# Nine pairs of chunks instead of five with the up product from 15 products of thirds

## The chip, the cores and the metric

The kernel runs on one core of one Trainium2 chip. The metric is device time in microseconds (us) of one execution. The profile of one execution is read beside it: when each instruction ran on each engine, and what ended each wait.

## The reference

The program is a gated linear recurrence followed by a mixer. Batch is 4, heads 8, sequence 768, head size 48; all data are float32. The recurrence, with the complex gate `a` limited to a magnitude of 0.999:

```python
for t in range(S):
    ar, ai = (a_re_n[:, :, t, :, None], a_im_n[:, :, t, :, None])
    new_re = ar * S_re - ai * S_im
    new_im = ar * S_im + ai * S_re
    kv = np.einsum('bhd,bhe->bhde', k[:, :, t], v[:, :, t])
    S_re, S_im = (new_re + kv, new_im)
    y[:, :, t] = np.einsum('bhd,bhde->bhe', q[:, :, t], S_re)
```

Its output, heads side by side, is `x` with 768 tokens of 384 numbers per batch. The mixer:

```python
xt = x.transpose(0, 2, 1)
h = xt @ U @ V                                  # over the tokens, rank 32
u = x + h.transpose(0, 2, 1)
ch = np.maximum(u @ w_ch1, 0.0) @ w_ch2         # 384 -> 1536 -> 384
return (u + ch).astype(np.float32)
```

## The kernel before

**Tiling.** The tokens are cut into 24 chunks of 128 (6 to a batch). Attention works on chunks. Two chunks form a gate group (12 groups, 0 to 11), and from group 5 on the products of a group's two chunks are issued together. The mixer works on pairs of chunks, `m` = 0 to 11, three to a batch. Since the rank product needs a batch's six chunks, a batch's mixing follows its attention and runs beside the attention of the next batch.

**Order.** Nothing is scheduled at run time. Every step is added to a plan with its engine and a stage, and the table `ORDER` gives each step, by engine and stage, its place in one long list (2671 places). The steps are issued in that order; each engine then works in order and waits on semaphores. The table `SPARE` puts fill matmuls of the identity, which compute nothing that is used, ahead of some places (`idle`, L1519; one unit is 128 columns, and a fill is left out where no PSUM tile is free).

**Gates.** ScalarE and VectorE turn a group's gates into magnitudes and angles (`magnitudes_of`, `turns_of`, `angles`, `waves`), with the tables of ScalarE switched twice a group. The sign of the real part becomes 1/pi with that sign, by bit operations on VectorE (L678), for the groups in `BITS` (0 to 2); for groups 3 to 11 ScalarE takes a Sign (with the constant `tiny`), and a second ScalarE step scales the angle and adds a quarter (with `fourth`). From group 3 on the values are split into two rounded parts for TensorE (`GS`). Sums over blocks of tokens ("tot", L741) and prefix products ("es ps", "ef ps", "ph") go through TensorE.

**Attention of a chunk.** `prep` weights queries and keys (`qk`), multiplies them by cosine and sine into `QKC` (two tiles, each head's two halves of 48 padded to 64 columns, so that a head takes 112 rows once transposed: `DQ` = 64 + 48). TensorE transposes them ("tr", L860), ScalarE copies them to `QK` (L871), of which there are three tiles. `chain` then scales `QK` in place by decays (`T`, VectorE), forms the blocks of the attention matrix ("inner", "corners"), the states ("dk", L996, `G`, `GM`), and reads out `y` (L1027, L1035) into `xo`, of which there are eight tiles.

**Mixing of a pair.** The rank product, `mixed` onto `xo`, a transpose to `uT` (L1107, L1111), then the up product into `h`, then the down product:
- *Up, plain* (`up`, L1122): pairs 0 to 6. Six steps, each with two row blocks of the weight and three parts of the contraction, 36 matmuls of 256 columns. ScalarE reads each step's PSUM with a relu into `h`.
- *Up, by thirds* (`up_fewer`, L1222): from pair `FEWER` = 7 on. The weight is cut into 3 x 3 blocks and `uT` into 3 x 2, and 15 products of sums of such blocks give the six thirds of the output. Each product is four matmuls of 128 columns. Four chains of partial sums run in PSUM (A and B long, C, D, E short). After every product its third is read: by a ScalarE copy the first time (L1230), later by VectorE, which adds it onto `h` (L390) and takes the relu with the last one (L1234). VectorE forms the twelve sums of `uT` for each pair in `put` (L1194) and once, in `combine` (L1275), eight sums of weight blocks. Both kinds of sum are kept in the `GATE` area, which the gates no longer need by then, with two weight sums in `sums_w`.
- *Down* (`down`, L1313, for pair 0; `down_two`, L1356, for the others): seven products of halves with sums `S1`, `S2` that VectorE forms (L1348) in `HS`: four pieces left over in `stage` (three) and `more`. The results are added to `xo` (L390) and stored.

One mixing step of the down product is half a product, 0.98 us in the plan's own costs.

Of the kernel before, what the change touches and what calls it, by code (L numbers as in the profile page):

```python
# [18 lines left out]
CH = 128  # L19
# [20 lines left out]
        ("POOL", "load"): {0: [14], 1: [34], 1.5: [84], 2: [31]},  # L40
        ("DVE", "load"): {1: [58]},
# [6 lines left out]
        ("ACT", "gates"): {0: [1, 2, 4, 6, 7, 16, 17, 22, 23, 29, 28, 45, 70, 71], 1: [24, 27, 38, 39, 41, 42, 46, 47, 65, 64, 67, 68], 2: [129, 108,  # L48
# [10 lines left out]
        ("DVE", "gates"): {0: [5, 8, 13, 18, 19, 54, 49], 1: [30, 21, 40, 43, 44, 51, 50], 2: [111, 143, 156, 185, 169], 4: [277, 322, 323, 372, 356],  # L59
# [10 lines left out]
        ("ACT", "angles"): {0: [72, 86, 98, 100, 103], 1: [76, 106, 112, 114, 126], 2: [210, 231, 251, 240, 241, 242, 263, 269, 271], 4: [375, 395,  # L70
# [5 lines left out]
        ("DVE", "angles"): {0: [81, 89], 1: [87, 107], 2: [211, 232, 252], 4: [376, 402, 425], 6: [589, 597, 602, 612, 625, 626, 665], 8: [698, 716,  # L76
# [4 lines left out]
        ("DVE", "prep"): {0: [85, 104, 110], 1: [121, 128, 145], 2: [226, 250, 265], 3: [203, 304, 309], 4: [373, 424, 427], 5: [443, 470, 472], 6:  # L81
# [159 lines left out]
def kernel(  # L241
# [19 lines left out]

    nc = tc.nc
    B, H, S, D = q.shape
    DP = 64
    DQ = DP + D
    DM = H * D  # L270
    FF = moe_w_ch1.shape[1]
    R = moe_U.shape[1]
    KD = DM // 128
# [78 lines left out]
    def c_one(n):  # L352
        return 0.15 + 0.00052 * n
# [1235 lines left out]
```

## Time and profile before

| | us |
|---|---|
| runs (3) | 627.15, 628.55, 629.3; median 628.55 |
| profiled execution, from first to last instruction | 627.0 |
| TensorE busy (PE) | 609.9 |
| TensorE weight loads (PEld) | 526.2 |
| VectorE busy (DVE) | 499.7 |
| ScalarE busy (ACT) | 415.8 |
| GpSimd busy (POOL) | 38.1 |

The profiled execution has no time of its own beside its span; the runs are measured from outside the span. PE counts matmuls, whose ends are modelled, so that neighbours overlap and the row of a group is longer than its share of the time; PEld counts the loads of the fixed operand, which run under earlier matmuls. A row of a group reads: line, engine, operation, output<-input, shape, count | busy us, mean ns of one | idle time before it, and what ended that. A row of the timeline reads: start, duration, line, operation, count of instructions merged into the row. A row of the waits reads: who waited for whom: us in total, times, longest. f32 matmuls are two instructions each.

### The profile page before, as it was taken

The numbers are of one execution on the slowest core, as the hardware profiler recorded it, in microseconds if no ns is written. First come the engines' busy times: TensorE is split into PE (matmuls) and PEld (weight loads), VectorE is DVE, ScalarE is ACT, GpSimd is POOL, SyncE is SP. The second block draws the span as 40 slices with busy tenths as digits, with TensorE's granted clock in tenths as the row PEclk, the third lists the DMA queues.
The fourth block names the chain that finished last, engine by engine and source line by source line (L and its number), as shares of the span: only waits on it lengthen the run. The fifth ranks groups of instructions, "written<-read, shape, count | busy, mean of one in ns | idle before, by whom it ended". The sixth has DMA issues, their size and how long they took to land.

```text
span 627.0 us, 23447 instructions
## 1 busy us (share of the span) xinstructions
PE 609.9 (97%) x10380; PEld 526.2 (84%) x10380; DVE 499.7 (80%) x887; ACT 415.8 (66%) x807; POOL 38.1 (6%) x79
## 2 busy tenths in 40 slices
PE   6998989999999999999999999999999999999998
PEld 3566767666889889889989989888999998999997
DVE  6899999888999979758977867788989884464554
ACT  6999999999898988687787867688433431202010
POOL 5000000000001010010000100000100100000100
PEclk7999999999999999999999999999999999999999
DMA  8864565644143252541512512601203020000101
GB/s 211 191 146 115 135 136 132 155 111 104 33 80 76 50 120 44 99 89 28 99 37 46 113 40 46 124 19 25 63 21 60 9 51 3 1 1 1 45 14 44
DMA packets 173685, 45.74 MB, mean 73 GB/s; under 512 B 167632, under 2 KB 170384, under 8 KB 173584
## 3 DMA queue, kind: packets, MB, share of 16 engines
q1 hardware_dynamic: 171376, 39.90, 30.1%
q0 software_dynamic: 2208, 4.35, 2.1%
q8 instruction: 81, 1.33, 0.9%
q14 instruction: 20, 0.16, 0.1%
HBM read 33.59 MB, written 4.72 MB: 61 GB/s over the span
## 4 chain that ended last, share of the span: by engine, by line
PE 77%; ACT 4%; DVE 3%; DMA 1%; issue 1%; SPq 0%; ACTq 0%; DVEq 0%
PE down L1356 24%; PE up L1122 15%; PE few L1222 11%; PE dk L996 3%; PE tr L860 3%; PE y L1035 3%; PE inner L910 2%; PE down L1313 2%; PE inner L907 2%; PE tot L741 2%; PE y L1027 2%; PE mixed L1089 2%; PE es ps L692 1%; PE ef ps L692 1%; PE uTp L1107 1%; PE corners L971 1%
## 5 line engine op out<-in xcount | busy, mean ns | idle before, releaser
L1122 PE MATMUL up<-uT,w 128*128 128x256 f32 x504 | 116.9, 383 | 0.0
L387 DVE TENSOR_TENSOR QK<-QK,T 112x512 f32<-112x512 f32 (+2 forms) x144 | 102.1, 732 | 8.4 <-PE inner L910 4.3
L1122 PEld LDWEIGHTS up<-uT,w 128*128 128x128 f32 x504 | 93.6, 190 | 12.5
L1356 PE MATMUL down<-w,h 128*128 128x192 f32 x396 | 72.2, 331 | 0.0
L384 ACT ACTIVATE gate<-gate 128x768 f32<-128x768 f32 (+1 forms) x82 | 64.8, 795 | 7.4 <-DVE GS L791 3.2
L1356 PEld LDWEIGHTS down<-w,h 128*128 128x128 f32 x396 | 64.1, 190 | 1.5 <-issue 0.7
L871 ACT COPY QK<-tr 112x512 f32<-112x512 f32 x96 | 51.2, 590 | 14.6 <-PE tr L860 14.3
L390 DVE TENSOR_TENSOR xo<-down,xo 128x192 f32<-128x192 f32 (+1 forms) x79 | 29.9, 387 | 27.5 <-PE down L1356 27.0
L387 DVE TENSOR_TENSOR QKC<-qk,cs 128x768 f32<-128x768 f32 x44 | 41.7, 955 | 6.3 <-ACT cs L384 3.6
L1230 ACT COPY h<-few 128x512 f32<-128x512 f32 x30 | 17.2, 586 | 40.8 <-PE few L1222 40.8
L1356 PE MATMUL down<-stage 128*128 128x192 f32 x198 | 37.6, 331 | 0.0
L1111 ACT COPY uT<-uTp 128x384 f32<-128x384 f32 x22 | 10.0, 479 | 41.4 <-PE uTp L1107 26.9
L1222 PE MATMUL few<-gate,w 128*128 128x128 f32 x280 | 34.8, 275 | 0.0
L1298 POOL DMA_DIRECT2D out_dram<-xo x32 | 19.2, 644 | 243.3 <-DVE xo L390 140.0
L860 PEld LDWEIGHTS tr<-ident,QKC 64*112 64x112 f32 x768 | 24.5, 130 | 10.7 <-issue 4.7
L1222 PEld LDWEIGHTS few<-gate,w 128*128 128x128 f32 x280 | 33.3, 192 | 0.0
L1356 PEld LDWEIGHTS down<-stage 128*128 128x128 f32 x198 | 32.1, 190 | 0.7 <-issue 0.2
L779 POOL DMA_DIRECT2D gate<-F x15 | 12.0, 799 | 327.9 <-DVE w L578 113.5
L860 PE MATMUL tr<-ident,QKC 64*112 64x64 f32 x768 | 29.4, 221 | 2.3 <-DVE QKC L387 1.6
L381 ACT ACT_TABLE_LOAD x24 | 30.8, 1283 | 1.1 <-PEq L1573 0.7
L384 ACT ACTIVATE h<-up 128x512 f32<-128x512 f32 x42 | 24.6, 596 | 9.8 <-PE up L1122 9.5
L976 ACT COPY AT<-corners 32x128 f32<-32x128 f32 x96 | 24.2, 255 | 9.6 <-PE corners L971 8.3
(200 smaller groups left out, 1285.4 us busy)
## 6 DMA issues: line engine op xcount, KB each, us to landing
stage<-in_moe_w_ch_dram SPq DMA_DIRECT2D x12, 768.0 KB, 5.0
qk<-in_q_dram SPq DMA_DIRECT2D x24, 192.0 KB, 3.2
qk<-in_k_dram SPq DMA_DIRECT2D x24, 192.0 KB, 2.7
VP<-in_v_dram SPq DMA_DIRECT2D x24, 192.0 KB, 3.6
gate<-in_a_re_dram SPq DMA_DIRECT2D x22, 192.0 KB, 3.4
gate<-in_a_im_dram SPq DMA_DIRECT2D x22, 192.0 KB, 3.4
AT<-DG SPq DMA_DIRECT2D x96, 32.0 KB, 2.3
T<-E SPq DMA_DIRECT2D x48, 48.0 KB, 2.9
```

The lines of the kernel that those rows point to most:

```text
L381: ACT(1.37, rank, lambda: nc.scalar.preload_act_table_set(name), writes=[TABLE])
L384: return nc.scalar.activation(out=o, in_=i, func=f, **kw)
L387: nc.vector.tensor_tensor(out=o, in0=a, in1=b, op=OP.mult)
L390: nc.vector.tensor_tensor(out=o, in0=a, in1=b, op=OP.add)
L860: nc.tensor.transpose(out=get(*ps[r])[0:DQ, h], in_=get(*qkc)[at, h].rearrange("p u d -> p (u d)")[:, 0:DQ], identity=ident[at, at], tile_ ...
L871: nc.scalar.copy(out=to, in_=a)
L976: ACT(0.36, RR, lambda r=r, u=u: nc.scalar.copy(out=get(*ATi).rearrange("p (a u) t -> p a u t", u=2)[r:r + BLK, :, u, BLK:2 * BLK], in_=ge ...
L996: nc.tensor.matmul(out=get(*dk[r])[x:end, h], lhsT=get(*ks)[at, h, x // DP, 0:end - x], rhs=get(*VPi)[at, h], start=True, stop=True, tile_ ...
L1122: nc.tensor.matmul(out=get(*ps)[:, e], lhsT=w1[:, f, (ff + e) * 128:(ff + e + 1) * 128], rhs=get(*uT)[:, f], start=(f == 0), stop=(f == KD ...
L1222: nc.tensor.matmul(out=get(*ps)[:, q], lhsT=w()[:, q * 128:(q + 1) * 128], rhs=v[0](), start=(n == 0 and q == 0), stop=True, skip_group_ch ...
L1298: queue.dma_start(out=out[b, c * CH:(c + 1) * CH, lo:hi], in_=get("xo", i)[:, lo:hi])
L1356: nc.tensor.matmul(out=get(*to)[:, part], lhsT=x(j), rhs=y[:, j], start=(first and j == 0), stop=(j == KH - 1), skip_group_check=not first)
```

## The change

1. `FEWER` = 3: pairs 3 to 11 form the up product by thirds, so four more pairs than before, 3 to 6.
2. Since the gates still need `GATE` at that time, the twelve operand sums go to `HS`, the tiles of the down product's sums, three to a piece. Seven of the eight weight sums go to `sums_w`, which grows from two to seven rows, and the eighth onto a block of `w1` that is not read any more; `combine` forms them in a slightly changed sequence.
3. The room comes from `QK`: two tiles instead of three, and 96 rows instead of 112. `QKC` holds a head's two halves of 48 next to each other (`DQ` = 96), with a short zeroed strip at the end, and the tiles `T` are no longer filled with ones at the start.
4. All groups take the sign by bits on VectorE. The ScalarE step that scaled the angle and added a quarter is gone: the quarter is added in the rounding steps (`angles`).
5. New code for `SUMMED` groups is there, but `SUMMED` is empty.
6. `ORDER` is new from the second batch's gates on (2770 places); `SPARE` loses its entries at places 514 to 551 and 664 to 678, 63 units in all; ten of these stood at places 514 and 518, ahead of group 3's block totals.

Places of some steps in the list:

| | before | after |
|---|---|---|
| transposes of chunk 14 | 1463, 1464 | 1509 on |
| last read-out of chunk 12, of chunk 13 | 1449, 1491 | 1483, 1533 |
| mixing of pair 3 | 1296 to 1502 | 1317 to 1504 |
| mixing of pair 6 | 1925 to 2122 | 2012 to 2159 |
| weight sums | 2018 to 2125 | 813 to 1287 |
| last read-out of chunk 23 | 2410 | 2512 |
| mixing steps of pair 8 ahead of it (of 29) | 20 | 22 |

The diff without `ORDER`:

```diff
-    DQ = DP + D
+    DQ = 2 * D
-    FEWER = B * (S // CH) // 2 - 5
+    FEWER = 3
...
-        QKC.append(singles.tile([128, H, 2, DP], FP, name="QKC%d" % n))
-        nc.gpsimd.memset(QKC[n][:, :, :, D:DP], 0.0)
+        QKC.append(singles.tile([128, H * DQ + DP - (DQ - DP)], FP, name="QKC%d" % n))
+        nc.gpsimd.memset(QKC[n][:, H * DQ:], 0.0)
...
-    sums_w = singles.tile([128, 2, KF // 3 * 128], FP, name="sums")
+    sums_w = singles.tile([128, 7, KF // 3 * 128], FP, name="sums")
...
-        nc.gpsimd.memset(TS[n], 1.0)
...
-            if g in BITS:
-                DVE(c_one(W), R1, lambda: nc.vector.tensor_scalar(out=t(n).bitcast(U32), in0=t(ar).bitcast(U32), scalar1=0x80000000,
-                                                                  scalar2=INV_PI, op0=OP.bitwise_and, op1=OP.bitwise_or), AR, [N])
-            else:
-                ACT(ca + 0.09, R1, lambda: act(t(n), t(ar), AF.Sign, bias=tiny), AR, [N])
+            DVE(c_one(W), R1, lambda: nc.vector.tensor_scalar(out=t(n).bitcast(U32), in0=t(ar).bitcast(U32), scalar1=0x80000000,
+                                                              scalar2=INV_PI, op0=OP.bitwise_and, op1=OP.bitwise_or), AR, [N])
...
-            if g not in BITS:
-                ACT(ca + 0.09, R2, lambda: act(t(z), t(z), AF.Identity, scale=1.0 / math.pi, bias=fourth), [], Z)
...
-                    ACT(c_act(DM), R2, lambda: nc.scalar.copy(out=of(a, i), in_=of(z, i)), [zi], [a + (i,)])
+                    ACT(c_act(DM) + 0.09, R2, lambda: act(of(a, i), of(z, i), AF.Identity, bias=fourth), [zi], [a + (i,)])
...
-                DVE(c_dve(DM), R2, lambda: nc.vector.tensor_tensor(out=of(b, i), in0=of(z, i), in1=of(a, i).bitcast(FP), op=OP.subtract),
-                    [zi, a + (i,)], [b + (i,)])
+                DVE(c_dve(DM), R2, lambda: nc.vector.scalar_tensor_tensor(out=of(b, i), in0=of(z, i), scalar=0.25, in1=of(a, i).bitcast(FP),
+                                                                          op0=OP.add, op1=OP.subtract), [zi, a + (i,)], [b + (i,)])
...
+    def turns_of_heads(qkc):
+        return get(*qkc)[:, 0:H * DQ].rearrange("p (h u d) -> p h u d", u=2, d=D)
...
-        buffer(QK, "QK", 3, [DQ, 5, H * HC])
+        buffer(QK, "QK", 2, [DQ, 5, H * HC])
...
         def mix_of(n):
-            return GATE[:, n, 0:KF // 3 * 128] if n < 6 else sums_w[:, n - 6]
+            return sums_w[:, n] if n < 7 else w1[:, 2, 0:KF // 3 * 128]
...
             def x(n, w=1):
-                at = n3 * 128 + n // 6 * CH
-                return GATE[:, n % 6, at:at + CH] if w == 1 else GATE[:, n:n + w, at:at + CH] if n < 6 else GATE[:, n - 6:n - 6 + w, at:at + CH]
+                a = HS[(2, 0, 1, 3)[n // 3]]
+                return a[:, n % 3] if w == 1 else a[:, n % 3:n % 3 + w]
 
             def x_of(n):
-                return "few", n % 6, "x%d" % (n // 6)
+                return "hs", (2, 0, 1, 3)[n // 3], n
...
-                S1, S2 = ("s1", 0, half), ("s2", 0, half)
+                S1, S2 = ("hs", half), ("hs", 2 + half)
```

More of the change, by code (lines that the diff above doesn't have):

```diff
@@ L171 @@
-        ("POOL", "angles"): {6: [615], 8: [708, 733], 10: [882, 931], 12: [1097], 14: [1273, 1302], 16: [1472, 1516], 18: [1669], 20: [1879, 1913],
-        22: [2039, 2077]},
-        ("DVE", "mixing"): {7: [2018, 2019, 2021, 2030, 2032, 2024, 2040, 2102, 2108, 2115, 2120, 2125, 2027]},
[7 rows of a table added]
+        ('POOL', 'load'): {0: [14], 1: [34], 1.5: [84], 2: [31]},
+        ('DVE', 'load'): {1: [58]},
[6 rows of a table added]
+        ('ACT', 'gates'): {0: [1, 2, 4, 6, 7, 16, 17, 22, 23, 29, 28, 45, 70, 71], 1: [24, 27, 38, 39, 41, 42, 46, 47, 65, 64, 67, 68], 2: [129, 108,
[10 rows of a table added]
@@ L174 @@
+        2003], 6: [2341, 2221, 2344], 7: [2419, 2302, 2436], 8: [2650, 2603, 2620], 9: [2656, 2618, 2658], 10: [2722, 2680, 2698]},
+        ('POOL', 'angles'): {6: [614], 8: [706, 731], 10: [861, 900], 12: [1076], 14: [1258, 1285], 16: [1505, 1565], 18: [1771], 20: [1950, 1976],
+        22: [2218, 2270]},
+        ('DVE', 'mixing'): {3: [930, 992, 1074, 1091, 1101, 813, 1006, 1031, 1126, 1279, 1283, 1284, 1287]},
 }
 SPARE = {20: 8, 32: 9, 62: 1, 66: 1, 73: 1, 82: 5, 91: 1, 113: 6, 116: 1, 119: 8, 140: 8, 153: 6, 157: 4, 167: 1, 168: 1, 207: 6, 216: 1, 217: 1, 282:
-         1, 352: 2, 436: 1, 514: 5, 518: 5, 527: 4, 546: 4, 547: 25, 551: 12, 596: 2, 601: 1, 606: 3, 624: 1, 632: 3, 646: 1, 653: 1, 664: 1, 672: 2,
@@ L301 @@
     PL = H * HC
-    BITS = range(SPLIT[0])
     PUT = (0, 2), (4, 6), (8, 10)
@@ L443, in w2_of @@
         return w2.rearrange("p (j x) m -> p j x m", x=2)[:, :, x, y * DH:(y + 1) * DH]
-    leps, lmax, tiny = column("leps", math.log(1e-6)), column("lmax", LNMAX), column("tiny", 1e-30)
+    leps, lmax = column("leps", math.log(1e-6)), column("lmax", LNMAX)
     magic, fourth, quarter = column("magic", MAGIC), column("fourth", 0.25), column("quarter", math.pi / 2)
@@ L655, in magnitudes_of @@
             table(ca, R1, lambda: act(t(y), t(y), AF.Ln, bias=1.0), [], Y)
-            if on_dve:
+            if g in SUMMED or g in SPREAD:
                 DVE(c_one(W), R1, lambda: nc.vector.tensor_scalar(out=t(l), in0=t(l), scalar1=-0.5, scalar2=-LNMAX, op0=OP.mult,
                                                                   op1=OP.max), [], [L])
-                DVE(cd, R1, lambda: add(t(l), t(l), t(y)), Y, [L])
+                if g not in SUMMED:
+                    DVE(cd, R1, lambda: add(t(l), t(l), t(y)), Y, [L])
             else:
@@ L685, in within @@
         def within(i, R1, L):
-            ps, es = ("es ps", i), ("es", i)
+            ps, es, parts = ("es ps", i), ("es", i), (y, l) if g in SUMMED else (l,)
             def summed(m, name, to, keeps):
@@ L695, in summed, with each @@
                 else:
-                    PE(0.65, R1, lambda: nc.tensor.matmul(out=get(*to), lhsT=m.bitcast(FP), rhs=of(l, i), start=True, stop=True),
-                       [L, name], [to, ("sums", g, i)], takes=[keeps], steps=2)
+                    def each():
+                        for u, a in enumerate(parts):
+                            nc.tensor.matmul(out=get(*to), lhsT=m.bitcast(FP), rhs=of(a, i), start=(u == 0), stop=(u == len(parts) - 1))
+                    PE(0.65 * len(parts), R1, each, [L, name] + [y + (i,)] * (g in SUMMED), [to, ("sums", g, i)], takes=[keeps], steps=2 * len(parts))
             psum(ps, "T", [128, DM], [128, 512])
@@ L726, in of_blocks @@
             lo = first
-            ps, e = ("tot", i), ("E", g)
+            ps, e, parts = ("tot", i), ("E", g), (y, l) if g in SUMMED else (l,)
             psum(ps, "T", [128, HH, NTOT])
@@ L734, in sums @@
                         h, w = at + (u * HH + p) * D, 64 if u == 0 else D
-                        nc.tensor.matmul(out=get(*ps)[u * 64:u * 64 + w, p], lhsT=get(*l)[:, h:h + w], rhs=total, start=True,
-                                         stop=True, tile_position=(0, u * 64))
+                        for n, a in enumerate(parts):
+                            nc.tensor.matmul(out=get(*ps)[u * 64:u * 64 + w, p], lhsT=get(*a)[:, h:h + w], rhs=total, start=(n == 0),
+                                             stop=(n == len(parts) - 1), tile_position=(0, u * 64))
             def at_once():
@@ L744, in of_blocks @@
             else:
-                PE(0.51, R1, sums, [l, ("total", 0), ("sums", g)], [ps], way=1, takes=[e], steps=4 * HH)
+                PE(0.2 + 0.31 * len(parts), R1, sums, [l, ("total", 0), ("sums", g)] + [y + (i,)] * (g in SUMMED), [ps], way=1, takes=[e],
+                   steps=4 * HH * len(parts))
             used = 2 * D if g in SPLIT else 64 + D
@@ L994, in state @@
                     at = slice(r * HC, (r + 1) * HC)
-                    for x, end in ((0, DP), (DP, DQ)):
-                        nc.tensor.matmul(out=get(*dk[r])[x:end, h], lhsT=get(*ks)[at, h, x // DP, 0:end - x], rhs=get(*VPi)[at, h],
+                    for x, w in ((0, DP), (DP, D)):
+                        nc.tensor.matmul(out=get(*dk[r])[x:x + w, h], lhsT=get(*ks)[at, h * DQ + x:h * DQ + x + w], rhs=get(*VPi)[at, h],
                                          start=True, stop=True, tile_position=(r * HC, x))
@@ L1169, in mix_of @@
         def mix_of(n):
-            return GATE[:, n, 0:KF // 3 * 128] if n < 6 else sums_w[:, n - 6]
+            return sums_w[:, n] if n < 7 else w1[:, 2, 0:KF // 3 * 128]
         def c_of(n):
-            return ("few", n, "w") if n < 6 else ("few", 0, "w%d" % n)
+            return "sums_w", n
         def up_fewer():
@@ L1275, in put @@
                 DVE(c_dve(n3), RC, lambda: nc.vector.tensor_tensor(out=c(n), in0=x(), in1=y(), op=op),
-                    [("w1", f) for f in range(KD)] + [c_of(k) for k in reads], [c_of(n)] + [("few", "b")] * (n == 3))
+                    [("w1", f) for f in range(KD)] + [c_of(k) for k in reads], [c_of(n)] + [("w1", 2, 0)] * (n == 7))
             sub_, add_ = OP.subtract, OP.add
@@ L1382, in down_two @@
             onto(ub, 0, two, 1)
-            product(one, 0, lambda j: of_s(2, j), W2S[1], lambda half: [("s2", 0, half)], first=False)
+            product(one, 0, lambda j: of_s(2, j), W2S[1], lambda half: [("hs", 2 + half)], first=False)
             onto(ua, 1, one, 0)
@@ L1388, in down_two @@
             sums(3, 1)
-            product(two, 0, lambda j: of_s(0, j), W2S[0], lambda half: [("s1", 0, half)])
+            product(two, 0, lambda j: of_s(0, j), W2S[0], lambda half: [("hs", half)])
             onto(ub, 1, two, 0)
@@ L1394, in down_two @@
             leave(0, 0)
-            product(two, 0, lambda j: of_s(2, j), w2_of(1, 1), lambda half: [("s2", 0, half)], first=False)
+            product(two, 0, lambda j: of_s(2, j), w2_of(1, 1), lambda half: [("hs", 2 + half)], first=False)
             onto(ua, 1, two, 0)
@@ L1467 @@
                 ring((nm, i), nm, EF)
-            ring(("few", n), nm, EF)
-            ring(("few", "b"), nm, EF)
-        else:
-            ring(("few", n), "g" + nm, [GATE[:, n]])
     waits, later, done = [], [], 0
```

56 lines of the change are left out of this document (27 added, 29 removed), and 246 rows, old and new, of the table ORDER.

## The prediction

> **What bounds the kernel now.** I read the page first: its busy line, then the chain that ended last.
>
> ```profile
> span 627.0 us, 23447 instructions
> PE 609.9 (97%) x10380; PEld 526.2 (84%) x10380; DVE 499.7 (80%) x887; ACT 415.8 (66%) x807; POOL 38.1 (6%) x79
> PE 77%; ACT 4%; DVE 3%; DMA 1%; issue 1%; SPq 0%; ACTq 0%; DVEq 0%
> PE down L1356 24%; PE up L1122 15%; PE few L1222 11%; PE dk L996 3%; PE tr L860 3%; PE y L1035 3%; PE inner L910 2%; PE down L1313 2%; PE inner L907 2%; PE tot L741 2%; PE y L1027 2%; PE mixed L1089 2%; PE es ps L692 1%; PE ef ps L692 1%; PE uTp L1107 1%; PE corners L971 1%
> ```
>
> TensorE carries the chain and is busy nearly always, but a busy TensorE may be pipelining slowly, so next I asked what TensorE itself waited for. The two longest entries:
>
> ```profile
> PE es ps L696 <- DVE GL L390: 3.8, 1, 3.8
> PE tr L860 <- DVE QKC L387: 1.6, 4, 0.8
> ```
>
> The 3.8 us is one wait at the start; everything else is a microsecond or two. Then I cut the span into stretches, because the engines do not share the load evenly. The columns are length, busy time of each engine, granted clock, DMA share and GB/s; 526 us is where the last chunk's read-out ends.
>
> ```profile
> core 0: us, PE busy (x) PEld busy (x) DVE busy (x) ACT busy (x) POOL busy (x), PEclk, DMA share, GB/s
> 20.00:120.00 100.00, 93.19 (x2168) 68.52 (x2166) 97.67 (x153) 96.55 (x188) 0.00 (x0) 1.00 0.60 143
> ...
> 160.00:220.00 60.00, 60.00 (x1280) 53.80 (x1279) 57.05 (x94) 54.40 (x107) 2.66 (x4) 1.00 0.33 64
> ...
> 440.00:526.00 86.00, 86.00 (x1758) 81.47 (x1758) 75.32 (x149) 31.59 (x77) 4.08 (x7) 1.00 0.17 37
> 160.00:526.00 366.00, 365.61 (x7070) 329.42 (x7070) 303.37 (x534) 256.17 (x513) 22.34 (x35) 1.00 0.30 59
> 526.00:626.00 100.00, 97.97 (x747) 94.75 (x742) 50.29 (x114) 14.34 (x28) 4.81 (x9) 1.00 0.05 17
> ```
>
> Three regimes. Up to 120 us VectorE (97.67 of 100) and ScalarE (96.55) are the limit. From 160 to 526 us attention and mixing run together and TensorE is the limit (365.61 of 366), with VectorE at 303.37/366 = 82.9%. In the tail only the mixer is left: TensorE full, VectorE half idle. Pairs 3 to 6, whose up product changes, lie in the middle regime. So TensorE work saved there is time saved, as long as VectorE, which pays for it, stays under its limit.
>
> **The up product, on TensorE.** Two pieces of the chain, each an unbroken run of one kind, with the time and the number of instructions:
>
> ```profile
> 325.83 7.77 PE up L1122 x36
> ...
> 463.96 7.14 PE few L1222 x64
> ```
>
> An `up` instruction (256 columns) takes 7.77/36 = 0.216 us, a `few` instruction (128 columns) 7.14/64 = 0.1116 us. Every f32 matmul is two instructions. The old form is 6 x 2 x 3 = 36 matmuls, 72 instructions, 15.54 us a pair; the new one 15 x 4 = 60 matmuls, 120 instructions, 13.39 us. That is 2.15 us a pair, 8.6 us for pairs 3 to 6. Pairs 7 to 11 have this form already.
>
> Per column the short instruction is 3% dearer (0.872 against 0.843 ns), which is in these numbers. [...]
>
> **The up product, on VectorE.** The groups of the existing thirds (five pairs), and four rows of the timeline:
>
> ```profile
> L1234 DVE CUSTOM_DVE_ANT_1 h<-few,h 128x512 f32<-128x512 f32 x30 | 20.3, 688 | 8.6 <-PE few L1222 8.0
> L390 DVE TENSOR_TENSOR h<-few,h 128x512 f32<-128x512 f32 x15 | 10.3, 690 | 17.2 <-PE few L1222 15.7 <-ACT QK L944 1.0 <-ACT F L384 0.5
> L1194 DVE TENSOR_TENSOR gate<-uT 128x128 f32<-128x128 f32 (+2 forms) x30 | 10.0, 353 | 1.3 <-ACT uT L1111 1.3
> L1194 DVE TENSOR_TENSOR gate<-gate,uT 128x128 f32<-128x128 f32 x10 | 2.9, 290 | 0.2
> L1194 DVE TENSOR_TENSOR gate<-uT,gate 128x128 f32<-128x128 f32 x5 | 1.4, 288 | 0.0
> ```
>
> ```profile
> 459.55 0.28 DVE L1194 TENSOR_TENSOR gate<-gate,uT 128x128 f32<-128x128 f32 x1
> 459.75 0.29 DVE L1194 TENSOR_TENSOR gate<-uT 128x128 f32<-128x128 f32 x1
> ...
> 460.82 0.89 DVE L1194 TENSOR_TENSOR gate<-uT 128x256 f32<-128x256 f32 x2
> ...
> 474.01 1.29 DVE L387 TENSOR_TENSOR QK<-QK,T 112x512 f32<-112x512 f32 x2
> ```
>
> By busy time a pair costs (20.3 + 10.3 + 10.0 + 2.9 + 1.4)/5 = 9.0 us. In a full queue an instruction starts before its predecessor's row ends: 0.20 us apart for 128 columns, 1.29 - 0.69 = 0.60 for 512. So nine folds of 512 cost 5.4, seven sums of 128 cost 1.4, and the two wider ones 0.89: 7.7 us. Since the queue will be full, I take 7.7, 31 us for four pairs (bounds 31 and 36). ScalarE swaps six relu reads of 512 columns for six copies of the same size: nothing. The thirteen weight sums only move from pair 7 to pair 3, still inside the 366 us.
>
> **The gate steps.** For groups 3 to 11 two ScalarE steps go and one VectorE step comes:
>
> ```profile
> L384 ACT ACTIVATE gate<-gate,tiny 128x768 f32<-128x768 f32 x9 | 8.4, 938 | 0.0
> L384 ACT ACTIVATE gate<-gate,fourth 128x768 f32<-128x768 f32 x9 | 8.4, 931 | 2.3 <-DVE gate L760 2.1
> L678 DVE TENSOR_SCALAR w<-w 128x768 uint32<-128x768 uint32 x1 | 0.6, 554 | 0.0
> ```
>
> ScalarE loses 16.8 us, VectorE gains 9 x 0.55 = 5.0, of which eight (4.4) fall behind 160 us. The quarter turn moves into the rounding steps at the same widths: nothing. ScalarE is no limit in the middle (256.17 of 366), so its gain hides there; a step of 0.93 us less on each group's way to its angles can only help. Group 3 lies in the first regime: between -1.9 (ScalarE's two) and +0.6 (VectorE's one); I take nothing.
>
> **Rows in 96, two query-key tiles, fillers, constants.** VectorE and ScalarE work along the free size, which stays, so 112 partitions or 96 cost the same; transposes lose 16 of 112 weight columns under unchanged 64 moving ones.
>
> ```profile
> L860 PEld LDWEIGHTS tr<-ident,QKC 64*112 64x112 f32 x768 | 24.5, 130 | 10.7 <-issue 4.7
> ```
>
> At most 16/112 of these 24.5 us, 3.5, could go, if the load were the limit; I take nothing. The removed fills and `tiny` stand at the start, where TensorE waits for the data instead: nothing. Of the dropped filler entries (63 units) nearly all never ran:
>
> ```profile
> 104.73 1.47 PE L741 MATMUL tot<-total,GL 128*96 128x32 f32 x16
> 106.03 0.60 PE L692 MATMUL ef ps<-GS,fore 128*128 128x384 f32 x2
> ...
> 137.06 0.49 PE L1519 MATMUL ef ps<-ident 128*128 128x128 f32 x2
> ```
>
> The entries of 10 units ahead of the two block totals show no filler there; the pair at 137.06 is what really goes. Nothing.
>
> **The sum.** By the lists of places, TensorE has done 20 of pair 8's 29 mixing steps before chunk 23's last read-out now, 22 after, about 2 us moved from tail to middle. The middle becomes 366 - 8.6 + 2 = 359.4 us for TensorE. VectorE has there 303.4 + 31 + 4.4 + 1 (its part of those two steps) = 339.8 us, 94.5%. From 160 to 220 us TensorE was full with VectorE at 57.05/60 = 95.1%, so this can be held. But a queue so full answers late: I charge 2.6 us for TensorE waiting on folds and operands (bounds 0 and 9, below), leaving 6.0. Span 627.0 - 6.0 = 621.0; the median of the runs, 628.55, lies 1.55 above the span, so **622.5 us**, with 620 to 626 as this case's own range.
>
> **Rivals.** *VectorE becomes the bound (slower).* The place is the middle; the time is 339.8 divided by the share that VectorE can reach, plus 259 outside. It decides below 339.8/359.4 = 94.5% and costs more than the gain below 339.8/368 = 92.3%. The rows give 95.1% (160 to 220 us) and 75.32/86 = 87.6% (440 to 526, where nothing forced more). Halfway, 91.3%, gives 372 + 259 = 631 span, 632.5 us; the lower end would be 647 span. For it: in-order queues of two full engines that feed each other. Against: 97.67 of 100 in the first regime shows that VectorE can run gapless. [...] I give it 0.20, since TensorE's own waits say that it is fuller than its loads show.
>
> *The new home of the operand sums costs the gain (no change).* They now share tiles with the down product's sums. Today the last down product of a pair runs between the next pair's last thirds:
>
> ```profile
> 606.42 1.14 PE L1356 MATMUL down<-w,stage 128*128 128x192 f32 x6
> 607.40 1.05 PE L1222 MATMUL few<-gate,w 128*128 128x128 f32 x8
> 608.29 1.14 PE L1356 MATMUL down<-w,more 128*128 128x192 f32 x6
> 609.26 1.05 PE L1222 MATMUL few<-gate,sums 128*128 128x128 f32 x8
> ```
>
> That cannot stay: six of twelve sums must wait until this product has read `stage` and `more`, and behind them in VectorE's queue wait the folds that free the thirds' PSUM. Pairs 3 to 11 have nine such junctions; about 1 us each (one step of TensorE, 607.40 - 606.42, with nothing to put in its place) is 9 us: 629 us. The two query-key tiles would add to the same loss: transposes of chunk 14 stand today at places 1463 and 1464, ahead of chunk 13's last read-out at 1491. Against: the sums that the first thirds need lie in the tiles that come free two products earlier, 4 x 0.98 = 3.9 us. 0.15.
>
> *All is kept and more.* Nothing lost of 8.6, and half of the nine ScalarE steps of 0.93 us on the angles' way come out as time: 628.55 - 8.6 - 4 = 616 us. 0.10.
>
> **How the numbers follow.** The forecast has 0.55. The measurement tells 0.3%, 1.9 us, from no change. Faster: 0.55, 0.10 and the upper edge of the other two, 0.05, together 0.70; same 0.12 from the shared tiles; slower 0.18, nearly all from VectorE. The range runs from the case where all is kept, 616, to the halfway price of VectorE's case, 632, and leaves out its worse half and a still larger gain.
>
> **What would show it.** Right: `up` with 216 instructions, `few` with 1080; `few` at 0.11 us in the middle too; the last read-out near 519.5 us; VectorE at 94 to 95% from 160 us to there; TensorE's waits for VectorE grown by 2 to 3 us. Wrong: a read-out after 526 us with VectorE below 92%, and TensorE waiting at `few` or at the transposes for VectorE (the slow rival); gaps at `few` behind L1194 at each pair's start, in the tail as well (the shared tiles); waits as few as today (all kept).

## The result, and the profile after

The changed kernel takes 624.84 us (median of 20 runs, 622.84 to 629.86) against 628.72 us (20 runs, 626.49 to 631.39) of the kernel before: a ratio of 0.994, with a 95% interval of 0.9925 to 0.9954. That is 3.9 us faster. The forecast was 622.5 us, with 616 to 632. The profiled execution of the changed kernel, with a span of 625.1 us and a time of 626.94 us, is among the slower of its runs.

The page after; the lines are the span, the engines' busy time, and the chain that ended last, by engine and by line:

```profile
span 625.1 us, 23940 instructions
PE 605.1 (97%) x10572; PEld 529.3 (85%) x10572; DVE 533.5 (85%) x967; ACT 402.0 (64%) x789; POOL 36.1 (6%) x76
PE 80%; ACT 8%; DVE 5%; DMA 3%; issue 2%; SPq 1%; ACTq 0%; DVEq 0%
PE down L1362 22%; PE few L1228 20%; PE up L1128 5%; PE tr L866 3%; PE dk L1002 3%; PE y L1041 3%; PE inner L916 3%; PE down L1319 2%; DMA gate<-F 2%; PE y L1033 2%; PE inner L913 2%; ACT gate L387 2%; PE tot L744 2%; PE mixed L1095 1%; PE up L1521 1%
```

TensorE still carries the chain. `up` fell from 15% to 5% of it and `few` rose from 11% to 20%. New in the list is `DMA gate<-F`, 2%: a transfer of 1.5 KB, with four pieces and 13.7 us of the chain, where the chain of before has two pieces and 5.7 us.

The stretches of after, in the columns that the prediction names (length, then busy time of TensorE, its weight loads, VectorE, ScalarE, GpSimd):

```profile
20.00:120.00 100.00, 92.60 (x2164) 67.97 (x2162) 97.55 (x153) 94.14 (x183) 0.00 (x0) 1.00 0.61 142
...
160.00:220.00 60.00, 59.55 (x1187) 52.73 (x1186) 57.75 (x98) 50.98 (x101) 2.12 (x3) 1.00 0.35 67
440.00:526.00 86.00, 86.00 (x1854) 81.62 (x1853) 76.09 (x145) 40.20 (x96) 5.48 (x9) 1.00 0.20 41
160.00:526.00 366.00, 362.82 (x7284) 335.18 (x7283) 336.14 (x615) 245.26 (x500) 22.41 (x35) 1.00 0.30 59
526.00:624.00 98.00, 96.11 (x720) 92.67 (x719) 50.62 (x113) 14.43 (x28) 4.32 (x8) 1.00 0.05 16
```

From 160 to 526 us VectorE rose by 33 us to 336.14/366 = 91.8%, and TensorE, full before (365.61), is now 3 us short of full (362.82). A full row is no proof of speed, since neighbours overlap: an `up` instruction of before is 383 ns long in the page, and the next one starts 216 ns after it does. So I also looked at the time from each TensorE instruction's start to the next one's, by kind. At the usual distance (the median in the trace, 216 ns for `up` and 112 ns for `few`) `up` needs 46.7 us instead of 108.9 and `few` 121.0 instead of 67.2, together 8.4 us less: the price of an instruction is as forecast. But the distances as they are, summed, fell from 111.8 to 48.2 us for `up` and rose from 68.2 to 127.5 us for `few`, together 4.3 us less. Of all that TensorE spends beyond the usual distances, the stretch from 240 to 280 us has 12.6 us, where it had 8.9.

**The place where it goes.** The waits of ScalarE after (who waited for whom, us in total, times, longest), and the DMA issue that they name (count, size, median us to landing):

```profile
ACT GS L387 <- DMA gate<-F: 12.1, 7, 3.3
```

```profile
gate<-F POOLq DMA_DIRECT2D x15, 1.5 KB, 3.2
```

The same two of before:

```profile
ACT GS L788 <- DMA gate<-F: 1.3, 2, 0.8
```

```profile
gate<-F POOLq DMA_DIRECT2D x15, 1.5 KB, 2.0
```

GpSimd's DMA carries a chunk's angle (1.5 KB) into the next chunk's gates; the rounding step on ScalarE waits for it. After, it waits seven times for 12.1 us, where it was twice for 1.3. Mostly that costs nothing. Once it does; the chain of waits after (start, us, what), the timeline of ScalarE, and that of TensorE:

```profile
265.15 4.67 DMA gate<-F
...
269.85 0.03 ACT GS L387
...
270.37 0.56 ACT QK L877
270.93 0.76 ACT uT L1117 x2
...
271.74 0.70 PE tr L866 x15
```

```profile
269.85 0.61 ACT L387 ACTIVATE GS<-gate,fourth 128x384 fp32r<-128x384 f32 x1 [2.77 <-DMA gate<-F]
270.37 0.56 ACT L877 COPY QK<-tr 96x512 f32<-96x512 f32 x1
270.83 0.85 ACT L1117 COPY uT<-uTp 128x384 f32<-128x384 f32 x2
```

```profile
268.54 1.14 PE L1362 MATMUL down<-w,h 128*128 128x192 f32 x6
271.36 1.07 PE L866 MATMUL tr<-ident,QKC 64*96 64x64 f32 x16 [1.68 <-ACT uT L1117]
272.37 2.08 PE L1228 MATMUL few<-stage,sums 128*128 128x128 f32 x8
274.23 1.72 PE L1228 MATMUL few<-stage,w 128*128 128x128 f32 x8
```

The transfer, issued at 265.15 us, takes 4.67 us. ScalarE stands at chunk 15's rounding step for 2.77 us. Behind it in ScalarE's fixed order stand copies that TensorE's next work needs: a chunk's transposed `QK` and pair 3's `uT`, whose PSUM TensorE wants back. TensorE stands 1.68 us, and then the two `few` rows of eight instructions take 2.08 and 1.72 us, where such a row takes 1.05 us in the prediction's lines. The clock column after, in steps of 2 us, says why:

```profile
270.00:272.00 2.00, 0.52 (x9) 0.39 (x11) 1.15 (x3) 2.00 (x5) 0.00 (x0) 1.00 0.02 5
272.00:274.00 2.00, 2.00 (x20) 1.87 (x17) 1.94 (x4) 1.96 (x4) 0.88 (x2) 0.55 0.00 0
274.00:276.00 2.00, 2.00 (x15) 1.88 (x15) 2.00 (x6) 0.88 (x3) 0.82 (x2) 0.60 0.61 199
```

The granted clock (third number from the end) fell to 0.55 and 0.60: half for 3.4 us in the trace's clock record (272.20 to 275.62 us), which by my estimate, half of 3.4, costs 1.7 us more. Not every run has this fall: five of the 20 show a granted clock of 1.00, and their median is 623.58 us.

### The profile page after: what moved, and what is told of

Read it like the earlier page. It is cut to its first block, busy times and chain, and to the rows that moved or that the text cites. A ratio compares the mean times of both kernels' runs of the same rounds, so it can differ in the third digit from the quotient of the medians.

```text
span 625.1 us, 23940 instructions
## 1 busy us (share of the span) xinstructions
PE 605.1 (97%) x10572; PEld 529.3 (85%) x10572; DVE 533.5 (85%) x967; ACT 402.0 (64%) x789; POOL 36.1 (6%) x76
## 4 chain that ended last, share of the span: by engine, by line
PE 80%; ACT 8%; DVE 5%; DMA 3%; issue 2%; SPq 1%; ACTq 0%; DVEq 0%
PE down L1362 22%; PE few L1228 20%; PE up L1128 5%; PE tr L866 3%; PE dk L1002 3%; PE y L1041 3%; PE inner L916 3%; PE down L1319 2%; DMA gate<-F 2%; PE y L1033 2%; PE inner L913 2%; ACT gate L387 2%; PE tot L744 2%; PE mixed L1095 1%; PE up L1521 1%
## 5 line engine op out<-in xcount | busy, mean ns | idle before, releaser
L390 DVE TENSOR_TENSOR QK<-QK,T 96x512 f32<-96x512 f32 (+2 forms) x144 | 102.3, 726 | 3.5 <-PE corners L977 1.1
L1236 ACT COPY h<-few 128x512 f32<-128x512 f32 x54 | 31.2, 589 | 46.9 <-PE few L1228 46.7
L877 ACT COPY QK<-tr 96x512 f32<-96x512 f32 x96 | 51.4, 583 | 10.7 <-PE tr L866 10.5
L1128 PE MATMUL up<-uT,w 128*128 128x256 f32 x216 | 50.6, 385 | 0.0
L1228 PE MATMUL few<-stage,w 128*128 128x128 f32 x360 | 47.9, 280 | 0.0
L1128 PEld LDWEIGHTS up<-uT,w 128*128 128x128 f32 x216 | 39.9, 190 | 5.8 <-DVE xo L393 0.3
L1228 PEld LDWEIGHTS few<-stage,w 128*128 128x128 f32 x360 | 44.4, 194 | 0.5
L1240 DVE CUSTOM_DVE_ANT_1 h<-few,h 128x512 f32<-128x512 f32 x54 | 36.3, 685 | 7.7 <-PE few L1228 6.2
L1228 PE MATMUL few<-stage,sums 128*128 128x128 f32 x288 | 38.9, 282 | 0.0
L1228 PEld LDWEIGHTS few<-stage,sums 128*128 128x128 f32 x288 | 35.6, 196 | 0.5
L866 PEld LDWEIGHTS tr<-ident,QKC 64*96 64x96 f32 x768 | 24.3, 123 | 12.1 <-DVE QKC L390 3.1
L866 PE MATMUL tr<-ident,QKC 64*96 64x64 f32 x768 | 29.8, 220 | 4.5 <-DVE QKC L390 1.8
```

The lines of the kernel that those rows point to most:

```text
L390: nc.vector.tensor_tensor(out=o, in0=a, in1=b, op=OP.mult)
L866: nc.tensor.transpose(out=get(*ps[r])[0:DQ, h], in_=get(*qkc)[at, h * DQ:(h + 1) * DQ], identity=ident[at, at], tile_position=(r * HC, 0))
L877: nc.scalar.copy(out=to, in_=a)
L1128: nc.tensor.matmul(out=get(*ps)[:, e], lhsT=w1[:, f, (ff + e) * 128:(ff + e + 1) * 128], rhs=get(*uT)[:, f], start=(f == 0), stop=(f == KD ...
L1228: nc.tensor.matmul(out=get(*ps)[:, q], lhsT=w()[:, q * 128:(q + 1) * 128], rhs=v[0](), start=(n == 0 and q == 0), stop=True, skip_group_ch ...
L1236: ACT(c_act(n3 * CH) - 0.045, RU, lambda i=i, k=k: nc.scalar.copy(out=at(i, k), in_=get(*ps)), [ps], [o])
```

## The experiments

Three theories stood against each other for what was lost. Theory 1: the up product's 8.6 us are saved, and the loss sits at 269 us, in ScalarE's fixed order behind the late transfer. Theory 2: VectorE's full queue answers late all along the middle. Theory 3: the operand sums, in shared tiles, cost time at each junction of two pairs. Every ratio is to the kernel before, run beside on the same chip (median 627.75 to 628.01 us), with its 95% interval; 0.01 is 6.3 us.

**1. The up product undone** (`few_plain`): all else of the change stays, pairs 3 to 6 are plain.

```diff
-    FEWER = 3
+    FEWER = 7
```

Their 15 places in `ORDER` were thinned to six, and five of the thirteen steps of the weight sums moved back behind pair 6's up product.

> The changed kernel with pairs 3 to 6 back on the plain up product, at places taken from their thirds; gate steps, rows of 96, two query-key tiles and the rest of the order stay. Theory 1 (the thirds save TensorE 8.5 us in full, and some 4.7 us are given back, for the most part by a ScalarE step that waits for the row-carry transfer near 265 us): 8 to 9 us above the changed kernel's 624.8, about 633, that is above the kernel before (628.7), since the wait near 265 us is in the order and stays. Theory 2 (VectorE's full queue makes TensorE wait all through the middle): the 31 us of VectorE go with the thirds, so only 3 to 5 us above, 628 to 630. Theory 3 (the operand sums' shared tiles): four of nine junctions go, 6 to 7 us above.

Measured: 635.65 us, ratio 1.0114 (1.0091 to 1.0136), 10.9 us over the changed kernel. The stretch, and ScalarE's wait, of this kernel:

```profile
160.00:526.00 366.00, 362.92 (x6919) 325.85 (x6917) 301.05 (x533) 242.02 (x492) 21.88 (x34) 1.00 0.30 58
```

```profile
ACT GS L401 <- DMA gate<-F: 8.6, 5, 4.1
```

VectorE is back at 301 us, and the time is no better for it. Theory 2 expected 628 to 630 us here. Undoing costs 2.3 us more than the 8.6 that the step was to bring, although TensorE's pause behind `uT` is only 0.27 us in this kernel. The rest may come from the thinned places, which nobody fitted, so this run does not measure the saving. The carry's wait is there without the new up product, so it does not come from the new products.

**2. The gate steps alone** (`gates_only`), on the kernel before:

```diff
-    BITS = range(SPLIT[0])
+    BITS = range(NG)
...
-            if g not in BITS:
-                ACT(ca + 0.09, R2, lambda: act(t(z), t(z), AF.Identity, scale=1.0 / math.pi, bias=fourth), [], Z)
...
-                    ACT(c_act(DM), R2, lambda: nc.scalar.copy(out=of(a, i), in_=of(z, i)), [zi], [a + (i,)])
+                    ACT(c_act(DM) + 0.09, R2, lambda: act(of(a, i), of(z, i), AF.Identity, bias=fourth), [zi], [a + (i,)])
```

> The kernel before with the gate part of the change alone: sign by bits on VectorE for all groups, the quarter turn in the rounding steps, two ScalarE steps fewer in groups 3 to 11, the new VectorE step at the place of the old ScalarE one. Theory 1 and the prediction: no effect, within 1 us of 628.7, ScalarE busy some 15 us less and VectorE some 4 us more. If the missing scaling step is what lays the row-carry transfer bare: 1 to 4 us slower, with ScalarE waiting over 5 us for that transfer (1.3 us before, 12.1 us after).

Measured: 628.14 us, ratio 0.9999 (0.9986 to 1.0012).

```profile
160.00:526.00 366.00, 365.16 (x7075) 329.03 (x7074) 305.14 (x539) 245.18 (x498) 22.40 (x35) 1.00 0.30 59
```

ScalarE has 11 us less in the middle, and the time does not move: to within a microsecond, this part of the change is worth nothing and costs nothing.

**3. The stalled copies ahead of the stalled step** (`act_order`), on the changed kernel. Chunk 15's rounding step, and VectorE's step after it, get later places, behind the copies of pair 3:

```diff
+ORDER["ACT", "angles"][14][3] = 1306.5
+ORDER["DVE", "angles"][14][3] = 1310.5
```

> The changed kernel with two steps moved in the order: chunk 15's rounding step on ScalarE, which waits for the row-carry transfer at 265 to 270 us, goes behind pair 3's two copies to uT, and its remainder step on VectorE behind the first operand sums. Theory 1: TensorE's 1.8 us of idling there and the fall of its clock to a half for 3.4 us (1.7 us) that follows in part of the runs go: 621.5 to 623.5, and no stretch at half clock behind 100 us. Theories 2 and 3: no change, 624.5 to 625.5.

Measured: 621.93 us, ratio 0.9899 (0.988 to 0.9918), 2.6 us under the changed kernel. The timeline of ScalarE in this kernel, and its stretches (the second ends with the last read-out):

```profile
267.22 0.86 ACT L1120 COPY uT<-uTp 128x384 f32<-128x384 f32 x2 [0.75 <-PE uTp L1116]
267.97 0.63 ACT L390 ACTIVATE GS<-gate,fourth 128x384 fp32r<-128x384 f32 x1
```

```profile
262.00:276.00 14.00, 14.00 (x226) 11.88 (x222) 12.69 (x27) 12.38 (x23) 2.46 (x4) 1.00 0.66 133
...
160.00:520.50 360.50, 359.36 (x7279) 332.28 (x7278) 334.67 (x613) 243.75 (x497) 22.37 (x35) 1.00 0.30 60
```

`uT` is copied as soon as TensorE has it; the rounding step then finds its transfer landed. TensorE is full from 262 to 276 us and its clock stays at 1.00. The last read-out ends at 520.5 us instead of 525.8. Two numbers in a list of 2770 places give back 2.6 us. How much of that is the pause, and how much the fall of the clock that only part of the runs have, was not told apart. This version beats both kernels.

**4. Half of the operand sums left out** (`no_late_sums`), on the changed kernel: six of the twelve in pairs 3 to 11, those that must wait for the previous pair's last down product.

```diff
+                if writes[0] in LATE:
+                    return
...
-                return (lambda: x(n)), (n,)
+                return u(n % 3, 0) if n in LATE else ((lambda: x(n)), (n,))
```

> The changed kernel without the six operand sums that lie in the two tiles that the last down product still reads (sums 0, 1, 2, 9, 10, 11): their products read blocks of uT instead, so this part of the up product is left out of the computation. About 1.1 us of VectorE a pair goes too, 10 us in all. Theory 3: TensorE has waited for these sums at nine junctions, so 3 to 8 us faster than 624.8. Theory 1: at most 1 us faster. Theory 2: 1 to 3 us faster, from the 10 us of VectorE.

Measured: 622.57 us, ratio 0.9907 (0.9889 to 0.9925), 2.1 us under the changed kernel. That looked like Theory 3. But the junctions touched by it are nine, and the profile of this kernel, of its slowest run, has the stall of 269 us once more, without the fall of the clock:

```profile
270.08 1.03 PE L871 MATMUL tr<-ident,QKC 64*96 64x64 f32 x16 [1.63 <-ACT uT L1122]
271.04 1.16 PE L1235 MATMUL few<-stage,sums 128*128 128x128 f32 x8
```

So the same sums were left out again where that stall is gone.

**5. Both** (`order_no_late`): 3 and 4 together.

> The reordered version without the six operand sums in the tiles that the last down product still reads (their products read blocks of uT; this part of the up product is left out). Theory 1: the 2 us that leaving them out gave without the reordering came for the most part through the same place near 269 us, so here at most 0.8 us below the reordered version's 621.9. Theory 3 (shared tiles): again 2 us or more, 620 or less. Theory 2 (VectorE's full queue): about 1 us, for 10 us of VectorE less.

Measured: 621.07 us, ratio 0.9892 (0.9875 to 0.991), 0.4 us under experiment 3 and inside its interval. Theory 3 falls: what the late sums cost beside the stall cannot be told from nothing. How they acted on the stall itself was not followed further.

**6. The next wait** (`act_sp_order`): in experiment 3 TensorE waited 0.7 us for a transfer `AT<-DG`; here, as well, one load on SP's queue gets another place.

```diff
+ORDER["SP", "load"][19][3] = 1262.5
```

> The reordered version (chunk 15's rounding step behind pair 3's copies to uT), with one more step moved: the gate load that the sync queue issues at 253.5 us, between two of the transfers that place chunk 12's and 13's diagonal blocks, goes behind them. TensorE waited 0.5 and 0.2 us for those transfers there. Theory 1: 0.3 to 1 us faster than the reordered version's 621.9, that is 621 to 621.6; if the placing transfers wait for something else than their turn in the queue, 621.9.

Measured: 621.35 us, ratio 0.9895 (0.9879 to 0.9912): not to be told from experiment 3.

**7 and 8. VectorE's load down and up** (`order_dve_less`, `order_dve_more`), on experiment 3. Down: the product of the keys with the end factor is left out from chunk 7 on. Up: the product of the keys by cosine and sine is made twice for chunks 7 to 21.

```diff
-            mul(a, a, heads(get("ef", i)).unsqueeze(2).to_broadcast([128, H, 2, D]))
+            if i < 7:
+                mul(a, a, heads(get("ef", i)).unsqueeze(2).to_broadcast([128, H, 2, D]))
```

```diff
+                for n in range(2 if 7 <= i < 22 and u else 1):
+                    mul(turns_of_heads(qkc), get(*qk)[:, u].unsqueeze(2).to_broadcast([128, H, 2, D]), get("cs", i))
```

> The reordered version without the product of keys and decay to the chunk's end from chunk 7 on (left out of the computation): 17 steps, 15 us of VectorE less in the middle, down to some 88% of it. Theory 1: at most 1 us faster than 621.9. Theory 2 (VectorE's full queue is what costs the rest): 2 to 8 us faster.

> The reordered version with the keys' product with cosine and sine done twice for chunks 7 to 21: 15 steps, 13 us of VectorE more, up to some 95.5% of the middle. The slow rival of the prediction (VectorE bound below 94.5%): 10 us or more slower than 621.9. Theory 1 (VectorE had 8% left, TensorE stays the bound): 1 to 4 us slower.

Measured: 622.46 us, ratio 0.9909 (0.9887 to 0.9931), and 632.71 us, ratio 1.0069 (1.005 to 1.0087). The middle of the two, and what TensorE waited for in the second (1.8 us, 5 times, in the changed kernel):

```profile
160.00:526.00 366.00, 364.17 (x7318) 335.82 (x7317) 322.28 (x599) 245.19 (x501) 22.37 (x35) 1.00 0.30 59
```

```profile
160.00:526.00 366.00, 357.26 (x7132) 328.96 (x7132) 346.34 (x624) 243.99 (x494) 21.82 (x34) 1.00 0.30 58
```

```profile
PE tr L870 <- DVE QKC L393: 7.1, 11, 1.1
```

14 us less on VectorE bring nothing: Theory 2 falls for the kernel of experiment 3. 13 us more cost 10.7, as if VectorE had become the bound between 91.8% and 94.6%, as the slow rival has it. But the added step stands just ahead of the transposes, so its lateness could be the price, whatever the load. Four more runs test the two.

**9. The same step twice where VectorE has room** (`before_dve_more`): the edit of experiment 8 on the kernel before.

> The kernel before, with the product of the keys by cosine and sine made twice for chunks 7 to 21 (the same values written twice; about 13 us more on VectorE, the same edit that cost about 10.7 us on the changed kernel with the earlier copies). Theory that VectorE's load is the price: VectorE goes from 303 to some 316 of 366 us, 86 %, still far below the place where it decides, so 0 to 2 us over the kernel before. Theory that the place is the price (the step stands ahead of the transposes, each doubling makes them 0.88 us later): 15 times 0.88 shows here as well, 8 to 12 us over the kernel before.

Measured: 634.94 us, ratio 1.0109 (1.0093 to 1.0125): 7 us, in a kernel whose VectorE is busy 85% of the middle.

```profile
160.00:526.00 366.00, 361.11 (x6982) 323.81 (x6980) 312.59 (x541) 254.87 (x508) 22.35 (x35) 1.00 0.30 59
```

**10. The load elsewhere** (`order_sums_twice`): on experiment 3, the operand sums of pairs 3 to 8 made twice.

```diff
-                DVE(c_dve(w * CH), RU, lambda: nc.vector.tensor_tensor(out=o(), in0=a(), in1=b(), op=op), [uT, ("w2s", 0)] + list(reads),
+                DVE(c_dve(w * CH), RU, lambda: [nc.vector.tensor_tensor(out=o(), in0=a(), in1=b(), op=op) for n in range(2 if 3 <= m < 9 else 1)], [uT, ("w2s", 0)] + list(reads),
```

> The changed kernel with the copies of pair 3 ahead of chunk 15's rounding step (621.9 us, ratio 0.9899), and every operand sum of pairs 3 to 8 made twice (the same values; nine instructions more a pair, about 2.3 us in a full queue, 14 us in six pairs). The sums stand ahead of the thirds of the up product and not ahead of the attention's transposes. Theory that VectorE's load is the price: VectorE comes to some 350 of 366 us, as with the doubled keys' product, and the time rises by 8 to 13 us, to 630 to 635 us. Theory that the place is the price: the sums have their tiles two products early, so 0 to 4 us, 622 to 626 us.

Measured: 632.82 us, ratio 1.0076 (1.0063 to 1.0089), 11 us over experiment 3, with VectorE busy for 348.57 of the 366 us. Each theory has one hit by now: experiment 9 speaks for the place, experiment 10 for the load (or for places just as tight).

**11 and 12. Late, but not loaded** (`order_more_less`, `order_sums_less`): experiments 8 and 10, each with the omission of experiment 7, so that VectorE's load is that of experiment 3 again.

> The changed kernel with the earlier copies (621.9 us, ratio 0.9899), the keys' product by cosine and sine made twice for chunks 7 to 21, and the product of the keys with the end factor left out from chunk 7 on: the kernel that cost 632.7 us (1.0069) with 15 us taken off VectorE again, behind the transposes of the same chunks. Theory that VectorE's load is the price of the added steps: the load is that of the kernel with the earlier copies, so 621 to 624 us, ratio 0.989 to 0.993. Theory that the lateness of the step in its fitted place is the price, whatever the load: 629 to 633 us, ratio 1.002 to 1.008.

> The changed kernel with the earlier copies, every operand sum of pairs 3 to 8 made twice, and the product of the keys with the end factor left out from chunk 7 on: the kernel that cost 632.8 us (1.0076) with 15 us taken off VectorE again. Theory that VectorE's load is the price: 621 to 624 us, ratio 0.989 to 0.993. Theory that lateness in a fitted place is the price: 629 to 633 us.

Measured: 629.59 us, ratio 1.0023 (1.0013 to 1.0034), and 630.41 us, ratio 1.0044 (1.0031 to 1.0057). The middle and TensorE's wait in experiment 11:

```profile
160.00:526.00 366.00, 359.08 (x7221) 331.23 (x7221) 334.19 (x611) 244.19 (x497) 22.36 (x35) 1.00 0.30 59
```

```profile
PE tr L870 <- DVE QKC L393: 6.6, 12, 1.1
```

The load is within 2 us of experiment 3's (336.06 us in the same stretch), and the time is 7.8 us longer. Against experiment 7, which has the same omission, the added steps cost 0.0114 and 0.0135 of the time, 7 and 8.5 us. So of the 10.7 us of experiment 8 some 7 stay when the load does not rise. By elimination I take them as the price of steps that come late in a fixed order, as large as in the kernel before; only the rest, 3.5 us (2.6 for the sums), goes with the load. Each of these is a difference of ratios, and their intervals together reach about 1.6 us either way for the first share and over 2 us for the second. That lateness costs more than load is likely from this; how much the load costs is hardly known. Where in the kernel before the 7 us arise was not followed: its TensorE's waits at the transposes grew by one microsecond only.

## Why the prediction came out right

**The up product on TensorE.** Forecast 8.6 us less; 8.4 at the usual distances of TensorE's instructions. `up` has 216 instructions and `few` 1080, as said. The page after has a short instruction 280 ns long, but the usual one still starts 0.11 us behind its predecessor:

```profile
L1128 PE MATMUL up<-uT,w 128*128 128x256 f32 x216 | 50.6, 385 | 0.0
L1228 PE MATMUL few<-stage,w 128*128 128x128 f32 x360 | 47.9, 280 | 0.0
```

As they stand in the order, the instructions bring less. From start to start, `up` and `few` together take 180.0 us before, 175.7 in the changed kernel, and 174.1 without the stall (experiment 3): 5.9 us less, and about 2.5 of the 8.4 are missing. They are no waiting for VectorE's load or for the late sums: with 14 us less on VectorE (experiment 7), and without the late sums (experiment 5), `up` and `few` take 174.0 us. The prediction took its price from an unbroken run. In the middle the thirds stand in shorter runs between attention's products (35 runs of `few` in the kernel, 18 before). Next to those the first or last distance of a run is mostly 0.20 to 0.21 us instead of 0.112; next to `down` it mostly stays at 0.11. The timeline of TensorE in experiment 3:

```profile
449.82 1.16 PE L1231 MATMUL few<-uT,sums 128*128 128x128 f32 x8
450.82 1.06 PE L1231 MATMUL few<-stage,sums 128*128 128x128 f32 x8
451.81 0.68 PE L1036 MATMUL y<-VP,AT 64*64 64x48 f32 x32
...
457.74 1.06 PE L1231 MATMUL few<-more,w 128*128 128x128 f32 x8
458.63 1.06 PE L1231 MATMUL few<-uT,sums 128*128 128x128 f32 x8
```

Eight instructions at the head of a run take 1.00 us to the next row's start, eight at its end 0.99, eight inside a run 0.89. The ends of the runs of both kinds hold 1.7 of the missing 2.5 us; why an end is dear is not shown.

**The up product on VectorE.** Forecast 31 us; the page after has 533.5 us busy against 502.9 with the pairs plain (experiment 1), 30.6.

**The gate steps, the rows of 96, the fillers.** Forecast nothing. Shown for the gate steps (experiment 2), though not in their terms: VectorE gained 1.8 us in the middle instead of 4.4, and a rounding step with the quarter in it takes 615 ns instead of 512. The rows of 96 and the fillers were not tried alone; a copy to `QK`, 512 columns in 96 rows, takes 583 ns, 590 in 112 rows before, where a copy of 512 columns in 128 rows took 586; VectorE's scaling of `QK` takes 681 ns, 687 before, where an addition onto `h` in 128 rows took 690. A weight load of these transposes takes 123 ns, 130 before.

**The middle.** Forecast 359.4 us long with VectorE at 94.5%, and the last read-out near 519.5 us. The profiled execution has 365.8 us and 91.8%, with the read-out ending at 525.8 us: taken alone, these signs were wrong. With the stall removed (experiment 3) they are 360.5 us, 334.67/360.5 = 92.8% and 520.5 us, which is near. But the forecast's 359.4 and 519.5 us leave out its own charge for waiting: with 2.6 us more they are 362.0 and 522.1, and neither kernel has that.

**The loss.** This is the step that failed, in its size and in its place. I charged 2.6 us for TensorE waiting on folds and operands. Of the saving of 8.6 us, 3.9 were left: 4.7 were lost. 2.6 of them come back when one step of ScalarE, with the VectorE step that follows it, is moved behind the copies of pair 3. TensorE's waits for VectorE did not grow by 2 to 3 us: at the transposes they went from 1.6 us in four waits to 1.8 in five. The prediction took ScalarE as no limit since it was busy for 256 of 366 us. But an engine in order needs no load to be late; one step that waits for a transfer is enough (2.77 us here), and I had not looked at what is queued behind it. Experiments 5 to 7 found the other 2.1 us neither in the operand sums, nor in the SP queue's place, nor in VectorE's load. In size they agree with the 2.5 us above, which `up` and `few` take beyond their usual distances; no run changed those alone. So the forecast came within 2.3 us of the result partly by luck: its charge was of a useful size, and the waits that it was charged for did not come.

**The rivals.** *VectorE becomes the bound*: not in this kernel (experiment 7). Its limit is not the wall that the prediction made of it either: at 94.6% the load's part of the price was some 3.5 us, where the rival's halfway price stood 10 us above the forecast. The prediction held TensorE for fuller than its loads show. After, the loads take 335.18 us of the middle, less than VectorE's 336.14, and still 14 us less of VectorE changed no time (622.46 us in experiment 7 against 621.93 in experiment 3). *The shared tiles*: VectorE did wait for them, TensorE did not, and leaving the late sums out saved 0.4 us (experiment 5). The lines of VectorE's waits after:

```profile
DVE stage L1200 <- PE down L1362: 4.7, 1, 4.7
...
DVE more L1200 <- PE down L1362: 1.3, 1, 1.3
```

*All kept and more*: the ScalarE steps on the angles' way are worth nothing (experiment 2), and no version came below 620.6 us in any run.

## What to carry to other kernels

In a kernel whose engines follow fixed orders, cost a change not only by load but by what stands behind each step that waits for a transfer: look at every in-order engine's longest waits for small DMAs, and put the steps that feed the bound ahead of them. Spare share of an engine is not free room: a step inserted ahead of the bound's input cost more than half its length at 85% load and at 91% (some 7 of 13 us in both), while the change's own 31 us on the same engine came with a new order and did not show. Price an instruction between the neighbours that it will have, and not from an unbroken run. To tell load from lateness, add the step and take as much work off the same engine elsewhere.

## What the runs showed of the hardware that was not expected

A TensorE pause of 1.68 us (269.68 to 271.36 us) was followed by half clock for 3.4 us in the changed kernel; in experiment 4 a pause of 1.63 us (268.45 to 270.08 us) at the same place was followed by none. Stretches of the changed kernel, then of experiment 4:

```profile
268.79:272.20 3.41, 1.61 (x22) 1.18 (x20) 1.28 (x4) 2.35 (x5) 0.00 (x0) 1.00 0.18 32
272.20:275.62 3.42, 3.42 (x22) 3.29 (x17) 3.42 (x8) 2.62 (x5) 1.70 (x3) 0.50 0.28 94
```

```profile
268.00:270.00 2.00, 0.45 (x3) 0.16 (x1) 0.56 (x1) 1.43 (x4) 0.00 (x0) 1.00 0.05 10
270.00:272.00 2.00, 1.80 (x24) 1.59 (x25) 1.80 (x5) 2.00 (x5) 0.16 (x1) 1.00 0.00 0
272.00:274.00 2.00, 2.00 (x42) 1.85 (x41) 2.00 (x5) 1.91 (x4) 1.54 (x3) 1.00 0.41 139
```

So after a pause of this length the clock fell once and once did not. In the changed kernel TensorE was busy for 1.61 of the 3.41 us that end with the fall; in experiment 4 it was busy for 0.45 + 1.80 = 2.25 us from 268 to 272 us, and the clock stays at 1.00. Why the two pauses end differently, and how little work makes the clock fall, is not shown. The trace of the kernel before has one piece at half clock, 6.83 us long, at its start (8.10 to 14.93 us).

A 1.5 KB transfer of GpSimd's queue took 2.0 us in the median before and 3.2 after, 4.67 at the stall. Six loads of 192 KB were issued on SP's queue between 261.06 and 266.17 us, around its own issue at 265.15. That they slowed it is argued from their place alone; no run here shows it.
